# Band attention before two dense layers: scores and outputs by pairs of 64-query units, on keys in place

## The chip, the core and the metric

One kernel runs on one of the eight cores of a Trainium2 chip. The metric is the device time of one execution in microseconds; lower is better. The engines of the core work side by side, each through its own queue in order: PE (matmuls; PEld is its weight loads), ACT, DVE and POOL (elementwise work) and SP, which here issues all DMAs.

## What is computed

`reference()` is attention of two batches, eight heads, 768 positions, head size 64, followed by two feed-forward layers on 1536 tokens of 512 channels. Each query sees the keys less than 16 positions away, and besides 24 summary keys: the maximum over each block of 32 keys, with the mean of the 32 values.

```python
k_sum = k.reshape(B, H, nb, block, D).max(axis=3)
v_sum = v.reshape(B, H, nb, block, D).mean(axis=3)
scores_l = np.where(np.abs(pos[:, None] - pos[None, :]) < 16, scale * q @ k.T, -1e9)
scores_s = scale * q @ k_sum.T + np.log(block)
a = softmax(concat([scores_l, scores_s])); attn = a @ concat([v, v_sum])
x = ((x @ w_a) * (x @ w_b)) @ w_out          # 512 -> 1536 -> 512
h = x @ w_in; out = (h - np.tanh(h)) @ w_out2  # 512 -> 2048 -> 512
```

The five weight matrices arrive as 64-bit floats.

## The kernel before

**Dense part.** Tokens go in three blocks of 512. Every operand of a dense product is split into a high and a low fp32r part, and a product of 128 rows of contraction is three matmuls of 512 columns. A list `pos` of positions, 12 matmuls each, is the backbone: per block and slice f of 128 hidden channels `pos_a`, `pos_b` and, one slice later, `pos_o` (positions 0 to 35 are block 0, 36 to 71 block 1); then `pos_h` and `pos_o2` for the second layer. A weight unit (512 KB of 64-bit words) is loaded into one of five buffers (`stage` three times, `x21a`, `x21b`), rebuilt as fp32 by two ACT copies (`dec_a`), a clamp on POOL and three DVE operations (`dec_b`), and split by one ACT and one DVE or POOL operation (`split_w`). `dec_b` issues the load of the next unit as it frees a buffer.

**Attention.** A unit u is 64 queries of all heads; a pair m is units 2m and 2m+1. `T1` transposes 128 queries and writes them as a block diagonal `qbd`: the two heads of a head pair p sit in the two halves of the rows and of the columns, zeros elsewhere, which takes two half copies. `W` copies a unit's 96 keys and the 24 summary keys to a tile `kw`, side by side. `T2m` makes a unit's scores, one 128 x 128 by 120 product for each p; rows 0 to 63 of the result are one head, rows 64 to 127 the other. `T2s`/`tt`, `ex` add the mask and take exponentials with their sums, `T2b`/`rb`, `nm` divide, `T3` transposes, `T4` multiplies by the values with eight 64-column products a unit and writes x, high part on ACT and low part on DVE.

**Order.** Units 0 to 7, the weights of positions 0 to 2 and the loads for them come first, in an order written by hand, the string `SEQ` (`LK`, `Lq`, `Lv`, `LV`, `Lw` are loads on SP; `da` to `df` rebuild a weight, `sh` and `sl` split it, `vc` copies the value means to a unit's value tile). Units 8 to 23 are planned into blocks 0 and 1 (`plan(j, ...)`), a unit every four positions. For positions below 72 a scheduler sets the order on PE, ACT, DVE and POOL, with attention given priority; SP keeps the order in which the program was written. A unit's values lie in `vw`, three buffers from unit 8 on: `load_v(u+3)` is planned right behind `T4(u)`, which frees its buffer, and what SP issues after it stands behind it.

Of the kernel before, what the change touches and what calls it, by code (L numbers as in the profile page):

```python
# [11 lines left out]
F32 = mybir.dt.float32  # L12
# [3 lines left out]
AF = mybir.ActivationFunctionType  # L16
# [23 lines left out]
def band_attention_moe_kernel(ctx: ExitStack, tc: tile.TileContext, q, k, v, w_a, w_b, w_out, w_in, w_out2, out):  # L40
# [36 lines left out]
    qbd2 = st([128, 2, NP, 128], "wsp", 4)  # L77
# [3 lines left out]
    qbd4 = st([128, 2, NP, 128], "wsp", 4)  # L81
    qbd3 = xb[:, 3072:4096].rearrange("p (u x c) -> p u x c", u=2, x=NP)

    def constants():
        nc.vector.memset(bsq, -math.sqrt(GA) * GB)
        nc.vector.memset(bth, -GC2)
        nc.vector.memset(qbd2, 0.0)
        nc.gpsimd.memset(qbd3, 0.0)
# [11 lines left out]
        nc.gpsimd.memset(qbd4, 0.0)  # L100
        for m, off in zip(masks, (0, WIN, 2 * WIN)):
# [89 lines left out]
    kwb = [st([128, NP, NK], "kw", 2) for _ in range(2)]  # L191
    kwb += [st([128, NP, NK], "w", 3 * F1) for _ in range(2)]
# [4 lines left out]

    def kw_of(u):
        if 8 <= u < 12:
            if u not in kwx:  # L200
                kwx[u] = st([128, NP, NK], "w", 3 * F1)
            return kwx[u]
        return kwb[u % 4 if u < 8 else u % 2]
# [61 lines left out]
    def T1(m, tag, qt):  # L265
        t = qn.pop(m)
        pp = pt(tag, (128, NP, 128))
        for p in range(NP):
            nc.tensor.transpose(pp[:, p, :], t[:, 2 * p : 2 * p + 2, :], ident)
        for h in range(2):  # L270
# [3 lines left out]
        for r in range(2):  # L274
            qb[2 * m + r] = qt[:, r]

    def W(u):
        b, w, k0 = where(u)
        kw = kw_of(u)
        nc.scalar.activation(kw[:, :, 0:KW], kt[b][:, :, k0 : k0 + KW], AF.Copy)  # L280
        if u < 14:
            nc.scalar.activation(kw[:, :, KW:NK], kt[b][:, :, S : S + NB], AF.Copy)

    def T2m(u, tag):
        qt, kw = qb.pop(u), kw_of(u)
        pp = pt(tag, (128, NP, 128))
        for p in range(NP):
            mm(pp[:, p, 0:NK], qt[:, p, :], kw[:, p, :], start=True, stop=True)  # L288
        at_x[u] = pp

    def T2s(u):
        b, w, k0 = where(u)
        pp = at_x[u]
        e = st([128, NP, NK], ("e", "ta", "tg")[u % 3] if u < 8 else "e", 2)
        nm = st([128, NP], "nm", 4)
        sm = st([128, NP], "sm", 4)
        mk = masks[0 if w == 0 else (2 if w == S // 64 - 1 else 1)]
        for p in range(NP):
            nc.vector.tensor_tensor_reduce(
                out=e[:, p, :], in0=pp[:, p, 0:NK], in1=mk, scale=-SC, scalar=3.0e38,  # L300
# [5 lines left out]
        at_x[u] = (e, sm)  # L306

    def T2(u, tag):
        T2m(u, tag)
        T2s(u)  # L310

    def T2b(u):
        e, sm = at_x[u]
        nc.vector.tensor_scalar(sm, sm, 1e-9, None, op0=ALU.add)
        nc.vector.reciprocal(sm, sm)
        if u % 2:
# [4 lines left out]
        at_x[u] = e  # L321

    def T3(u, tag, eng="act"):
        e = at_x.pop(u)
# [3 lines left out]
        at = st([NK, NP, 128], ("at", "gh", "gl")[u % 3] if u < 8 else "at", 2)  # L328
        if eng == "act":
            nc.scalar.activation(at, pp[0:NK], AF.Copy)  # L330
        else:
            nc.vector.tensor_copy(at, pp[0:NK])
        at_x[u] = at

    def T4(u, tag):
        at, vt = at_x.pop(u), vw_of(u)
        pp = pt(tag)
        for p in range(NP):
            for h in range(2):
                mm(  # L340
                    pp[h * 64 : (h + 1) * 64, p * 64 : (p + 1) * 64], vt[:, 2 * p + h, :], at[:, p, h * 64 : (h + 1) * 64],
                    start=True, stop=True,
                )
        x = X[u // 8]
        c0 = (u % 8) * 64
        src = pp[:, 0:256].rearrange("x (p c) -> x p c", p=NP)
        nc.scalar.activation(x[:, 0, :, c0 : c0 + 64], src, AF.Copy)
        nc.vector.tensor_tensor(x[:, 1, :, c0 : c0 + 64], src, x[:, 0, :, c0 : c0 + 64].bitcast(F32), op=ALU.subtract)  # L348
# [202 lines left out]
    for n, u in enumerate(range(8, 24)):  # L551
        j = (n - 8) * 4 + begin[1] + OFF if n >= 8 else n * (begin[1] // 8) + OFF
        b, w, _ = where(u)
        if u % 2 == 0:
            m = u // 2
            if m + 2 < 12:
                plan(j, load_q, m + 2)
            plan(j, T1, m, "pt", qbd)
            if u >= 12:
                plan(j, W, u)  # L560
                plan(j, W, u + 1)
        if u % 8 == 0:
            plan(j, new_x, u // 8)
        plan(j + 2, T2, u, "ps")
        plan(j + 3, T2b, u)
        plan(j + 5, T3, u, "pt")
        plan(j + 7, T4, u, "ps")
        if u + 3 < 24:
            plan(j + 7, load_v, u + 3)
            if 12 <= u + 3 < 15:  # L570
                plan(max(j + 7, VM + NC + 5), load_vm, u + 3)
# [263 lines left out]
```

## Time and profile before

| | us |
|---|---|
| median of three runs (lowest, highest) | 660.85 (659.47, 661.19) |
| the profiled execution | 659.97 |
| its span, from first to last instruction | 658.2 |
| PE busy, share | 637.4, 97% |
| DVE, ACT, POOL busy | 501.9, 475.1, 209.1 |
| mean granted PE clock | 0.995 of full |

The page's chain that ended last is 83% PE and 8% DVE. Its slices show PE at nine tenths or more from the fourth on, except one; DMA is near full over the first 100 us and near nothing after 365 us. A matmul's end is modelled, so the distance from one matmul's start to the next is the better measure of what PE spends.

### The profile page before, as it was taken

What the parts mean: (1) busy time and instruction counts of PE and PEld (TensorE: products, weight loads), DVE (VectorE), ACT (ScalarE), POOL (GpSimd) and SP (SyncE); (2) the same over time, 40 slices, a digit from 0 to 9 for tenths busy, and PEclk for the clock granted to TensorE, in tenths of its full rate; (3) what the DMA queues carried; (4) which work ended last, traced back from release to release, by engine and by line L of the source; (5) the groups of instructions that cost most, each with busy time, mean ns of one, the idle gap of its engine ahead of it and who ended that gap; (6) DMA issues with size and microseconds to landing.
All of it is one profiled execution on the core that took longest, in us unless ns stands there. A gap on an engine that the chain in (4) does not pass through costs nothing.

```text
span 658.2 us, 9626 instructions
## 1 busy us (share of the span) xinstructions
PE 637.4 (97%) x3240; PEld 518.2 (79%) x3240; DVE 501.9 (76%) x999; ACT 475.1 (72%) x1000; POOL 209.1 (32%) x221
## 2 busy tenths in 40 slices
PE   7779999999799999999999999999999999999997
PEld 5567876888588888888888888888888888888885
DVE  5889999898675777747877749777777877777775
ACT  4899886897686787645655548777777777777774
POOL 6752231222000011100111134554444554444441
PEclk9979999999999999999999999999999999999999
DMA  9996984563324554513444200000010000010001
GB/s 203 242 240 185 249 224 127 176 214 116 81 89 124 164 161 141 154 54 113 143 145 145 80 1 0 1 0 1 1 64 1 0 1 0 26 40 1 1 0 64
DMA packets 84781, 62.11 MB, mean 94 GB/s; under 512 B 51892, under 2 KB 75444, under 8 KB 84732
## 3 DMA queue, kind: packets, MB, share of 16 engines
q1 hardware_dynamic: 84732, 61.50, 33.3%
q8 instruction: 25, 0.41, 0.3%
q14 instruction: 24, 0.20, 0.1%
HBM read 54.00 MB, written 7.34 MB: 93 GB/s over the span
## 4 chain that ended last, share of the span: by engine, by line
PE 83%; DVE 8%; ACT 4%; DMA 2%; issue 2%; SPq 1%; POOL 0%; DVEq 0%; ACTq 0%
PE acc L459 20%; PE pb L370 18%; PE pa L370 17%; PE acc L398 12%; PE pt L370 5%; PE ps L370 5%; PE ps L288 1%; DVE w L164 1%; PE ps L340 1%; DVE wsp L185 1%; DMA stage<-in_moe_w_in_dram 1%; DVE w L165 1%; PE pt L240 1%; PE pt L327 1%; SPq L610 1%
## 5 line engine op out<-in xcount | busy, mean ns | idle before, releaser
L185 POOL TENSOR_TENSOR wsp<-w,wsp 128x512 fp32r<-128x512 f32 x97 | 127.4, 1330 | 140.0 <-ACT wsp L184 140.0
L184 ACT ACTIVATE wsp<-w 128x512 fp32r<-128x512 f32 x201 | 121.3, 622 | 17.8 <-PE acc L398 8.0
L185 DVE TENSOR_TENSOR wsp<-w,wsp 128x512 fp32r<-128x512 f32 x104 | 73.9, 712 | 41.0 <-ACT wsp L184 40.8
L179 POOL TENSOR_SCALAR w<-w 128x512 f32<-128x512 f32 x52 | 41.8, 809 | 181.7 <-ACT w L154 168.9
L398 PE MATMUL acc<-gh,wsp 128*128 128x512 f32 x288 | 96.5, 394 | 1.2 <-ACT gh L363 1.2
L370 PE MATMUL pa<-XA,wsp 128*128 128x512 f32 x336 | 85.2, 402 | 2.1 <-ACT XA L720 2.1
L370 PE MATMUL pb<-XA,wsp 128*128 128x512 f32 x336 | 83.9, 393 | 1.4 <-DVE tg L386 1.4
L459 PE MATMUL acc<-wsp,gh 128*128 128x512 f32 x256 | 78.8, 389 | 0.0
L370 PEld LDWEIGHTS pa<-XA,wsp 128*128 128x128 f32 x336 | 64.1, 193 | 16.6 <-ACT XA L720 2.4
L370 PEld LDWEIGHTS pb<-XA,wsp 128*128 128x128 f32 x336 | 62.1, 188 | 14.9 <-ACT x21a L155 1.7
L363 ACT ACTIVATE gh<-tg 128x512 fp32r<-128x512 f32 x68 | 42.4, 624 | 33.9 <-DVE tg L386 33.6
L398 PEld LDWEIGHTS acc<-gh,wsp 128*128 128x128 f32 x288 | 53.7, 188 | 11.9 <-ACT gh L363 1.3
L370 PE MATMUL pb<-XB,wsp 128*128 128x512 f32 x240 | 60.8, 396 | 0.0
L370 PE MATMUL pa<-XB,wsp 128*128 128x512 f32 x240 | 60.0, 394 | 0.0
L398 PE MATMUL acc<-gl,wsp 128*128 128x512 f32 x144 | 56.8, 396 | 1.1 <-DVE gl L364 1.1
L459 PEld LDWEIGHTS acc<-wsp,gh 128*128 128x128 f32 x256 | 48.1, 188 | 9.9
L364 DVE TENSOR_TENSOR gl<-tg,gh 128x512 fp32r<-128x512 f32 x68 | 46.8, 688 | 9.1 <-ACT gh L363 8.9
L370 PEld LDWEIGHTS pa<-XB,wsp 128*128 128x128 f32 x240 | 44.5, 188 | 9.4 <-DVE XB L348 0.2
L370 PEld LDWEIGHTS pb<-XB,wsp 128*128 128x128 f32 x240 | 44.4, 188 | 9.2
L459 PE MATMUL acc<-wsp,gl 128*128 128x512 f32 x128 | 49.8, 389 | 0.0
L459 PE MATMUL acc<-wsp,vw 128*128 128x512 f32 x192 | 46.5, 391 | 0.0
L459 PEld LDWEIGHTS acc<-wsp,vw 128*128 128x128 f32 x192 | 35.9, 188 | 8.2 <-ACT vw L363 0.4
(304 smaller groups left out, 1175.5 us busy)
## 6 DMA issues: line engine op xcount, KB each, us to landing
stage<-in_moe_w_out_dram SPq DMA_DIRECT2D x19, 512.0 KB, 3.5
stage<-in_moe_w_in_dram SPq DMA_DIRECT2D x16, 512.0 KB, 5.6
stage<-in_moe_w_a_dram SPq DMA_DIRECT2D x8, 512.0 KB, 5.0
w<-wsc SPq DMA_DIRECT2D x16, 256.0 KB, 3.4
vw<-in_v_dram SPq DMA_DIRECT2D x19, 192.0 KB, 3.0
stage<-in_moe_w_b_dram SPq DMA_DIRECT2D x7, 512.0 KB, 5.6
wsc<-x21a SPq DMA_DIRECT2D x8, 256.0 KB, 5.1
wsc<-x21b SPq DMA_DIRECT2D x8, 256.0 KB, 4.9
```

The lines of the kernel that those rows point to most:

```text
L164: nc.vector.scalar_tensor_tensor(r, t[:, :, 1], -0x40000000, r, op0=ALU.bitwise_and, op1=ALU.bitwise_or)
L165: nc.vector.tensor_tensor(r, r, t[:, :, 0], op=ALU.add)
L179: nc.gpsimd.tensor_scalar(rf, rf, HI_HI, HI_LO, op0=ALU.min, op1=ALU.max)
L184: nc.scalar.activation(s[:, 0, :], r, AF.Copy)
L185: eng.tensor_tensor(s[:, 1, :], r, s[:, 0, :].bitcast(F32), op=ALU.subtract)
L240: mm(pp, mavg[:, NB - 4 - 4 * c : 2 * NB - 4 - 4 * c], vch.pop(c).rearrange("p h d -> p (h d)"), start=(c == 0), stop=(c == NC - 1),)
L288: mm(pp[:, p, 0:NK], qt[:, p, :], kw[:, p, :], start=True, stop=True)
L363: nc.scalar.activation(dst[0], src, AF.Copy)
L364: eng.tensor_tensor(dst[1], src, dst[0].bitcast(F32), op=ALU.subtract)
L370: mm(dst, w, xx, start=(kk == 0 and n == 0), stop=(kk == KC - 1 and n == 2))
L398: mm(acc[blk][d][:, c0:c1], w, t, start=(f == 0 and c0 == 0 and n == 0), stop=(f == F1 - 1 and n == 2))
L459: mm(a[c], g[:, cs], s[:, i, :], start=(f == 0 and n == 0), stop=(f == F2 - 1 and n == 2))
```

## The change

- **Plain q copies.** `T1` writes the transposed queries with one copy of 128 x 512; the zeroed block-diagonal buffers and their memsets go.
- **Scores on keys in place.** `T2m` now works on a pair. A product is 64 rows (one head) by 64 columns (one unit's queries) by keys; heads go to two PSUM banks, units to the two halves of their rows. Keys are read from the transposed keys `kt` themselves, so that a unit needs two products, 96 keys and 24 summary keys. `W` stays for units 8 to 11 alone (`kwx`), with one product of 120.
- **By head, not by unit.** After `T2m` a tile of 128 rows holds one head of both units. `T2s`, `T2b`, `T3` run for (m, h) instead of u; their number is the same. Masks are made for pairs.
- **T4 and x by 128 tokens.** One bank takes a pair's sixteen products; one ACT and one DVE operation of 512 write x, instead of two of 256 each.
- **First order.** `SEQ` is new. Loads of weights stand among those of attention; the engine of several steps changes, and all `df` and `sl` of the first three weights go to POOL. `load_v` comes in twos behind `T4(m)`.

```diff
+    def q_of(m):
+        return qbx[:, m - 2] if m in (2, 3) else qbd[:, m % 2]
-    def T1(m, tag, qt):
+    def T1(m, tag):
...
-        for h in range(2):
-            r = slice(h * 64, h * 64 + 64)
-            dst = qt[r, :, :, h * 64 : h * 64 + 64]
-            nc.scalar.activation(dst, pp[r].rearrange("x p (u c) -> x u p c", u=2), AF.Copy)
+        nc.scalar.activation(q_of(m), pp, AF.Copy)
...
-        for p in range(NP):
-            mm(pp[:, p, 0:NK], qt[:, p, :], kw[:, p, :], start=True, stop=True)
+                if 2 * m + n in kwx:
+                    parts.append(((0, NK, kwx[2 * m + n]),))
+                else:
+                    parts.append(((0, KW, kt[b][:, :, k0 : k0 + KW]), (KW, NK, kt[b][:, :, S : S + NB])))
+            for i in range(len(parts[0])):
+                for h in range(2):
+                    r = slice(h * 64, h * 64 + 64)
+                    for n in range(2):
+                        c0, c1, keys = parts[n][i]
+                        mm(
+                            pp[h][n * 64 : n * 64 + 64, p, c0:c1], qt[r, p, n * 64 : n * 64 + 64], keys[r, p, :],
+                            start=True, stop=True,
+                        )
...
+    def T4m(m, tag):
+        at = [at_x.pop((m, h)) for h in range(2)]
+        pp = pt(tag, (128, NP, 128))
+        for n in range(2):
+            vt = vw_of(2 * m + n)
+            c = slice(n * 64, n * 64 + 64)
+            for p in range(NP):
+                for h in range(2):
+                    mm(pp[h * 64 : (h + 1) * 64, p, c], vt[:, 2 * p + h, :], at[h][:, p, c], start=True, stop=True)
+        return pp
...
+        x, c0 = X[m // 4], (m % 4) * 128
+        nc.scalar.activation(x[:, 0, :, c0 : c0 + 128], pp, AF.Copy)
...
-    for n, u in enumerate(range(8, 24)):
-        j = (n - 8) * 4 + begin[1] + OFF if n >= 8 else n * (begin[1] // 8) + OFF
+    for n, m in enumerate(range(4, 12)):
+        j = (n - 4) * 8 + begin[1] + OFF if n >= 4 else n * 2 * (begin[1] // 8) + OFF
...
+        plan(j + 9, T4, m, "ps")
+        for u in (2 * m + 3, 2 * m + 4):
+            if u < 24:
+                plan(j + 9, load_v, u)
...
-    T3E, WE, ADD, SPL, VCE = 'DDDDADDD', 'PPDPPDPP', 'PDD', 'PPD', 'APPPAPDD'
+    T1E, T3E, ADD, SPL, VCE = 'AADD', 'ADDDDAAA', 'PPP', 'PPP', 'DDDDPDPP'
```

Three places of the order. SP in the first order, before: the last value loads (`w`, `vw` from `in_v`), then the first weights.

```order
L620 DMA XA<-in_v_dram 128x8x128 x3
L258 DMA w<-in_v_dram 96x8x64 x5
L258 DMA vw<-in_v_dram 96x8x64 x3
L141 DMA stage<-in_moe_w_a_dram 128x4x256
L141 DMA stage<-in_moe_w_b_dram 128x4x256
```

The same place after:

```order
L620 DMA XA<-in_v_dram 128x8x128 x2
L246 DMA w<-in_v_dram 96x8x64
L138 DMA stage<-in_moe_w_b_dram 128x4x256
L246 DMA w<-in_v_dram 96x8x64 x3
L138 DMA stage<-in_moe_w_a_dram 128x4x256
L246 DMA w<-in_v_dram 96x8x64
L246 DMA vw<-in_v_dram 96x8x64 x2
L138 DMA stage<-in_moe_w_b_dram 128x4x256
L246 DMA vw<-in_v_dram 96x8x64
L140 DMA x21a<-in_moe_w_out_dram 128x1024
```

The last value load of the first eight units now stands behind the fourth weight load, the second one from `w_b`, which takes the first `stage` buffer again and so waits until `df0` has emptied it.

PE in block 0, before: a `T2` (L288), a `T4` (L340) and what stands around them.

```order
L398 MATMUL acc_884<-gh,wsp 128x512
L288 MATMUL ps<-kw,qbd 128x120 x4
L398 MATMUL acc_885<-gh,wsp 128x512
L370 MATMUL pb<-XA,wsp 128x512 x9
L340 MATMUL ps<-at,vw 64x64 x8
L370 MATMUL pb<-XA,wsp 128x512 x3
```

After, the scores of pair 6 begin as follows, and a `T4` stands in two parts:

```order
L287 MATMUL pt<-kt,qbd 64x96 x2
L287 MATMUL pt<-kt,qbd 64x24 x2
L376 MATMUL pb<-XA,wsp 128x512 x9
L332 MATMUL pt<-ident,e 120x128 x4
L345 MATMUL ps<-at,vw 64x64
L345 MATMUL ps<-at,vw 64x64 x15
```

Scores of a pair are now 32 products of 64 columns' weights (16 for pairs 4 and 5) in place of eight of 128. They stand in one piece, except for pairs 5 and 6, which are in two; `T4` of seven pairs is in two pieces, 1 and 15 products.

SP toward the end of block 0, before: a value load (L258) stands behind `T4` of one unit, and behind it the last weights of the first layer.

```order
L143 DMA x21b<-in_moe_w_out_dram 128x1024
L258 DMA vw<-in_v_dram 96x8x64
L143 DMA stage<-in_moe_w_out_dram 128x1024
L141 DMA stage<-in_moe_w_in_dram 128x4x256 x2
L258 DMA vw<-in_v_dram 96x8x64
```

After:

```order
L138 DMA stage<-in_moe_w_a_dram 128x4x256
L246 DMA vw<-in_v_dram 96x8x64 x2
L138 DMA stage<-in_moe_w_b_dram 128x4x256
L140 DMA x21a<-in_moe_w_out_dram 128x1024
L140 DMA x21b<-in_moe_w_out_dram 128x1024
L138 DMA stage<-in_moe_w_in_dram 128x4x256 x3
L246 DMA vw<-in_v_dram 96x8x64 x2
```

Two value loads now wait together for `T4` of pair 6, and three weights that block 0 still needs (for positions 33, 34 and 35) stand behind them; before it was one, for position 35, behind `T4` of unit 13.

## Rows read from the trace of the kernel before

**Rows 1.** Span and granted PE clock of the core.

```profile
core 0: 658.2 us, clock 0.995
```

**Rows 2.** Stretches: start:end, length, busy us (count) of each engine, clock, DMA share.

```profile
40.00:60.00 20.00, 16.43 (x68) 12.63 (x67) 17.88 (x35) 18.94 (x46) 6.53 (x8) 0.83 0.94 242
60.00:80.00 20.00, 20.00 (x116) 16.56 (x115) 18.41 (x40) 17.11 (x37) 4.05 (x6) 1.00 0.84 205
...
160.00:200.00 40.00, 36.56 (x204) 29.22 (x203) 26.34 (x70) 28.05 (x71) 3.09 (x5) 1.00 0.31 89
```

**Rows 3.** PE's timeline: start, length, group, [idle before <-what ended it].

```profile
42.48 5.74 PE L370 MATMUL pa<-XA,wsp 128*128 128x512 f32 x12 [2.11 <-ACT XA L720]
...
57.37 2.99 PE L370 MATMUL pb<-XA,wsp 128*128 128x512 f32 x12 [1.44 <-DVE tg L386]
...
169.93 1.21 PE L398 MATMUL acc<-gh,wsp 128*128 128x512 f32 x4 [1.21 <-ACT gh L363]
```

**Rows 4.** PE's timeline around a T2 and a T4, and in the second layer.

```profile
83.72 1.05 PE L288 MATMUL ps<-w,qbd 128*128 128x120 f32 x8
84.52 2.98 PE L370 MATMUL pa<-XA,wsp 128*128 128x512 f32 x12
87.34 0.61 PE L370 MATMUL pb<-XA,wsp 128*128 128x512 f32 x2
87.89 0.69 PE L340 MATMUL ps<-at,vw 120*64 120x64 f32 x16
88.50 2.56 PE L370 MATMUL pb<-XA,wsp 128*128 128x512 f32 x10
90.90 0.39 PE L398 MATMUL acc<-gh,wsp 128*128 128x512 f32 x1
...
501.25 2.88 PE L370 MATMUL pb<-XA,wsp 128*128 128x512 f32 x12
503.97 0.61 PE L459 MATMUL acc<-wsp,gh 128*128 128x512 f32 x2
```

**Rows 5.** PE's timeline in the first order: a T2 and two T4 in a row.

```profile
13.60 1.12 PE L288 MATMUL pt<-kw,qbd 128*128 128x120 f32 x8 [0.25 <-ACT qbd L599]
...
36.73 0.67 PE L709 MATMUL ps<-w,vw 120*64 120x64 f32 x16
37.20 0.67 PE L709 MATMUL pt<-gl,w 120*64 120x64 f32 x16
```

**Rows 6.** Timelines of DVE and POOL late in the first order.

```profile
37.20 1.13 DVE L757 SCALAR_TENSOR_TENSOR w<-stage,w 128x512 int32<-128x512 int32 x1
40.77 0.69 DVE L757 SCALAR_TENSOR_TENSOR w<-stage,w 128x512 int32<-128x512 int32 x1
42.46 0.42 DVE L722 TENSOR_TENSOR XA<-pb,XA 128x256 fp32r<-128x256 f32 x1 [1.00 <-ACT XA L720]
36.41 1.38 POOL L737 TENSOR_SCALAR w<-w 24x512 f32<-24x512 f32 x2
38.47 1.29 POOL L759 TENSOR_TENSOR w<-w,stage 128x512 int32<-128x512 int32 x1 [0.68 <-POOL w L737]
```

**Rows 7.** DMA issues by line: count, size of one, median us to landing.

```profile
vw<-in_v_dram SPq DMA_DIRECT2D x19, 192.0 KB, 3.0
stage<-in_moe_w_b_dram SPq DMA_DIRECT2D x7, 512.0 KB, 5.6
```

**Rows 8.** SP's own waits: us in total, times, longest.

```profile
SPq L258 <- PE ps L340: 112.6, 11, 20.5
```

**Rows 9.** Chain of waits ahead of 168 us: start, us, what.

```profile
156.28 6.25 DMA stage<-in_moe_w_in_dram
```

**Rows 10.** Groups by line and form: busy us, mean ns of one, idle before.

```profile
L280 ACT ACTIVATE kw<-kt 128x384 f32<-128x384 f32 x12 | 6.2, 517 | 0.0
L273 ACT ACTIVATE qbd<-pt 64x512 f32<-64x512 f32 x16 | 9.4, 590 | 0.9 <-PE pt L269 0.8
```

More of the change, by code (lines that the diff above doesn't have):

```diff
@@ L76, in band_attention_moe_kernel @@
     qbd = st([128, 2, NP, 128], "qbd")
-    qbd2 = st([128, 2, NP, 128], "wsp", 4)
+    for _ in range(4):
+        st([128, 2, TB], "wsp", 4)
     xb = st([128, 2 * KC * TB], "XB")
     kq = xb[:, 0:3072].rearrange("p (c h d) -> p c h d", c=NC, h=H)
-    qbd4 = st([128, 2, NP, 128], "wsp", 4)
-    qbd3 = xb[:, 3072:4096].rearrange("p (u x c) -> p u x c", u=2, x=NP)
+    qbx = xb[:, 3072:4096].rearrange("p (u x c) -> p u x c", u=2, x=NP)
     def constants():
@@ new lines, in W, with T2m @@
+        nc.scalar.activation(kwx[u][:, :, 0:KW], kt[b][:, :, k0 : k0 + KW], AF.Copy)
+        nc.scalar.activation(kwx[u][:, :, KW:NK], kt[b][:, :, S : S + NB], AF.Copy)
+    def T2m(m, tags):
+        qt = q_of(m)
+        pp = [pt(t, (128, NP, 128)) for t in tags]
+        for p in range(NP):
+            parts = []
+            for n in range(2):
+                b, w, k0 = where(2 * m + n)
+                if 2 * m + n in kwx:
[12 more added lines that the diff above has]
+        for h in range(2):
+            at_x[m, h] = pp[h]
@@ L305, in T2s, with T2, T2b @@
             )
[L306 to L313, printed above, removed]
+        at_x[m, h] = (e, sm)
+    def T2(m, tags):
+        T2m(m, tags)
+        for h in range(2):
+            T2s(m, h)
+    def T2b(m, h):
+        e, sm = at_x[m, h]
         nc.vector.tensor_scalar(sm, sm, 1e-9, None, op0=ALU.add)
         nc.vector.reciprocal(sm, sm)
-        if u % 2:
+        if h:
             nc.vector.tensor_tensor(e, e, sm.unsqueeze(2).to_broadcast([128, NP, NK]), op=ALU.mult)
@@ L327, in T3, with T4 @@
             nc.tensor.transpose(pp[0:NK, p, :], e[:, p, :], ident)
[L328 to L337, printed above, removed]
-        for p in range(NP):
[L339 to L348, printed above, removed]
+        at = st([NK, NP, 128], "at", 2)
+        nc.scalar.activation(at, pp[0:NK], AF.Copy)
+        at_x[m, h] = at
+    def T4m(m, tag):
+        at = [at_x.pop((m, h)) for h in range(2)]
+        pp = pt(tag, (128, NP, 128))
+        for n in range(2):
+            vt = vw_of(2 * m + n)
+            c = slice(n * 64, n * 64 + 64)
+            for p in range(NP):
+                for h in range(2):
+                    mm(pp[h * 64 : (h + 1) * 64, p, c], vt[:, 2 * p + h, :], at[h][:, p, c], start=True, stop=True)
+        return pp
+    def T4(m, tag):
+        pp = T4m(m, tag)
+        x, c0 = X[m // 4], (m % 4) * 128
+        nc.scalar.activation(x[:, 0, :, c0 : c0 + 128], pp, AF.Copy)
+        nc.vector.tensor_tensor(
+            x[:, 1, :, c0 : c0 + 128], pp, x[:, 0, :, c0 : c0 + 128].bitcast(F32), op=ALU.subtract
+        )
     xtag = ["XA", "XB"]
@@ L550, in band_attention_moe_kernel @@
     OFF = -2
-    for n, u in enumerate(range(8, 24)):
-        j = (n - 8) * 4 + begin[1] + OFF if n >= 8 else n * (begin[1] // 8) + OFF
[L553 to L571, printed above, removed]
+    for n, m in enumerate(range(4, 12)):
+        j = (n - 4) * 8 + begin[1] + OFF if n >= 4 else n * 2 * (begin[1] // 8) + OFF
+        if m + 2 < 12:
+            plan(j, load_q, m + 2)
+        plan(j, T1, m, "pt")
+        if m % 4 == 0:
+            plan(j, new_x, m // 4)
+        plan(j + 2, T2, m, ("ps", "pt"))
+        for h in range(2):
+            plan(j + 3 + h, T2b, m, h)
+            plan(j + 5 + 2 * h, T3, m, h, "pt")
+        plan(j + 9, T4, m, "ps")
+        for u in (2 * m + 3, 2 * m + 4):
+            if u < 24:
+                plan(j + 9, load_v, u)
+                if 12 <= u < 15:
+                    plan(max(j + 9, VM + NC + 5), load_vm, u)
     for d in range(KC):
@@ L701, in op @@
             cp(T3E[i], t, P_["T3", i][0:NK])
[L702 removed]
+            at_x[divmod(i, 2)] = t
         elif n.startswith("T4m"):
             i = int(n[3])
[L705 to L713 removed]
+            P_["T4", i] = T4m(i, tg())
         elif n.startswith("T4"):
```

109 lines of the change are left out of this document (33 added, 76 removed).

## The prediction

> **What bounds the kernel now.** I read the span and clock first. The span is 658.2 us [rows 1], the profiled execution 659.97, so 1.8 lie around it, and that execution is 0.9 under the median of 660.85, well inside the runs. Then the table of stretches [rows 2]: PE is busy for 20.00 of 20.00 us from 60 to 80. From 40 to 60 it is idle for 3.57, at a granted clock of 0.83, and from 160 to 200 it is idle for 3.44; the slices of the page show no other hole after the head. So from about 57 us the kernel costs what PE issues, plus one gap. ACT (17 to 19 of 20 us) and DVE (18) are nearly full in block 0, but PE does not wait for them except in that gap, which begins with gh of ACT [rows 3]. Before 57 us PE is mostly a server of the attention chain, and the end of that head is set by when x of the first 512 tokens is complete: pa(0) starts at 42.48 behind ACT writing `XA`, pb(1) at 57.37 [rows 3].
>
> A matmul's end is modelled, so I price PE by distances of starts. Twelve matmuls of 512 columns take 503.97 − 501.25 = 2.72 us, 0.227 each, 0.444 ns a column [rows 4]. A `T2` among them: 84.52 − 83.72 = 0.80, and the twelve behind it need 87.34 − 84.52 = 2.82 instead of 2.72; the visit costs 0.90. A `T4`: from 87.34 to 90.90 are twelve pb and one `T4`, 3.56 − 2.72 = 0.84. Two `T4` in a row start 0.47 apart for 16 instructions [rows 5], 29 ns each, which is 64 columns at 0.444. So of a visit's 0.84, 0.47 is products and 0.37 is the way into the small form and out of it. The same rows show each fp32 product as two passes: 16 instructions for eight products.
>
> **Part one: PE after the head.** This is where every microsecond counts in full.
>
> Scores of pairs 6 to 11 are 32 products, 64 passes. The 32 passes of 96 columns take 96 × 0.444 = 43 to 44 ns, 1.40 us. The 32 of 24 columns would take 11 ns by columns, but each needs its own weights of 64 columns, and the shortest cadence with new weights in the trace is the 29 ns of `T4` [rows 5]; I take 29, 0.93 us. With 0.37 for the visit that is 2.70 a pair, against two visits of 0.90 = 1.80: +0.90 for each of six, **+5.4**.
>
> Pairs 4 and 5 have 32 passes of 120 columns, 54 ns each: 1.74 + 0.37 = 2.11 against 1.80, twice, **+0.6**. Two visits of scores are split in two (pairs 5 and 6): **+0.7**.
>
> `T4`: before 16 visits of 0.84, 13.4. After 8 × 32 × 29 ns = 7.5, and 15 visits (seven are split) of 0.37 = 5.6, together 13.1: **−0.4**.
>
> Sum **+6.3**. Transposes keep their number. Bounds of the one unknown, the cadence of these products: by columns alone the short passes give back 0.59 a pair, −3.5, so +2.8; if two neighbours ran fully at once, products halve (6 × 1.17 + 2 × 0.87 = 8.7), −2.4; if each pass waited for its weights as long as it runs, products double, +17.5, so +23.8. I take the middle value because `T4` [rows 5] is nearest: 64 columns of weights, fp32, small form, in one order on one engine.
>
> **Part two: what is hidden.** ACT loses most of the unit copies `W` (12 of them, 6.2 us [rows 10]) and half of its copies of q (16 of 0.59, 9.4 us [rows 10], become 8 of a little more), and writes x once a pair: some 10 us of ACT in the main part, and a little of DVE. PE at 20.00 of 20.00 hides all of it; I cost it at nothing, and would count it only where ACT is the last releaser, in the gap at 168. Masks and sums by head instead of by unit are as many and as long. If that cover were gone, in the head, it counts there.
>
> **Part three: the head.** I walked the new first order through instruction by instruction, each on its engine in order, each waiting for its operands, with the durations of its line before; the same walk on the old order gives pa(0) at 42.3 where the trace has 42.48, so it is good to a few tenths. A score visit is 2.3 there (a row of `T2` starts as early as 13.60 [rows 5]). The steps that decide: four score pairs take about 9.3 us of PE, more than eight visits did, but the exponentials end within 0.2 us of where they did, since ACT and DVE are the slower part. All `df` go to POOL, 1.29 instead of 0.69 [rows 6]. That costs on POOL and frees DVE, with one more cost shown by the rows: a DVE operation that runs beside a POOL one takes 1.13 at 37.20 while POOL's 36.41 + 1.38 is under way, and 0.69 at 40.77 [rows 6]. In the walk `df0` ends at 35.3.
>
> The queue: the last value load now stands on SP behind a weight load that waits for `df0` to empty `stage`. So it is issued at about 35.3. The weight load alone takes 5.6 and the value load 3.0 [rows 7]; two together 4.7 by my estimate, bounds 3.0 (no contention) and 8.6 (one after the other). It lands at 40.0; unit 7's `T4`, 42.2; its high part on ACT, 42.8; its low part on DVE, 43.5 (before: 42.46 + 0.42 = 42.9 [rows 6]). pa(0) thus starts at **43.5 to 43.6**, 1.1 later. The twelve matmuls of pa(0) took 5.74 [rows 3], in part waiting for the split weights; at half clock 512 columns are 0.43, twelve 5.1. The split weights are all ready earlier now, `sl0` at 40.2, so that wait goes. Behind it pb(0), the next pa, scores of pair 4, and pb(1) at **56.4** against 57.37 [rows 3], with about the same PE work ahead of it: −1.0. Half of that I give to the error of the walk: **−0.5**, between −3 (the value load early, the clock full) and +4 (the value load last).
>
> **Part four: the gap at 168.** SP waited for 112.6 us in 11 times for `T4` before a value load, the longest 20.5 [rows 8], and what stands behind is held with it: a weight of w_in issued at 156.28 landed 6.25 later [rows 9]. Now two value loads and behind them the weights of positions 33, 34 and 35 wait for `T4` of pair 6, which stands at position 29.6 in PE's order; before, one weight, for position 35, waited for `T4` of unit 13 at 30.8. From there to position 33 are 3.4 positions of 2.72 and about 3 us of visits: some 12.5 us. The weight needs 6.25 to land and seven steps of decoding and splitting of 0.69 each [rows 6], 4.8: 11.1. Just in time; I leave the gap of 3.44 [rows 2] as it is.
>
> **Forecast:** 659.97 + 6.3 − 0.5 = **665.8**, by the profiled execution; its own range, by the cadence and the head, is 661.5 to 669.
>
> **The rivals.**
>
> *Four products at once* (faster). A product fills a quarter of the array, and neighbours use other quarters. The point from which it decides: a cadence under 22 ns averaged over the 64 passes of a pair ((1.80 − 0.37) / 64) would take the price below that of two `T2`. At half the cadence PE after the head gains 8.7 on the forecast, the head 1.9: **655.2**. Against it: `T4`'s neighbours already lie in two column halves [rows 5], and their starts are 64 columns apart, no less. The Trainium skill, "TensorEngine Tiling (Array Packing)", section "Key Properties", says that different tiles load and multiply in parallel; by that rule this rival would be the forecast, but the 29 ns do not show it for `T4`. Chance 0.13.
>
> *The paired value loads starve block 0* (slower). If the two value loads, 3.0 each [rows 7], go ahead of the weight one after the other, position 33 is ready after 6.0 + 6.25 + 4.8 = 17.0 us against 12.5: PE stands 4.5 more near 165 to 172 us, **670.3**. It decides if the weight is not split 12.5 us after `T4` of pair 6. For it: the longest waits are of this line [rows 8]. Against: DMA is at 0.31 there [rows 2]. Chance 0.18.
>
> *Loads of one row half do not overlap* (slower still). Both products of a head use the same 64 rows; if weights for a half of the rows only load when its products are done, three of four loads show: 0.75 × 17.5 = 13, **679**. Against it: `T4`'s weights all lie in the same rows and come every 29 ns [rows 5]. The Trainium skill, "TensorE: Matmul & The Clock Gate", section "The mechanism", says that weight loads overlap running products only where the row group differs; the 29 ns speak against that. Chance 0.06.
>
> *The gap closes and the clock holds* (same). With ACT some 10 us lighter gh is no longer late at 169.93 [rows 3], −3.4; and if PE, which has more to do in the head, keeps its full clock into pa(0) (before, half level from 41.6 to 48.4, the 0.83 of rows 2), twelve matmuls gain 12 × 0.2 = 2.4: **660.0**. One of the two alone leaves 662.4 or 663.4. For it: ACT is named as what ended that gap. Against it: its weights come through the same SP queue. Chance 0.20.
>
> **How the numbers follow.** Forecast 0.43, four at once 0.13, starved 0.18, no overlap 0.06, gap and clock 0.20. A measurement of this kernel can tell about 0.3% from no change, so same is 658.9 to 662.8. Slower: 0.58, of the forecast 0.34 and the two slower rivals, 0.18 and 0.06. Faster: 0.22, four at once and 0.09 of the last rival, below its figure. Same: 0.20, the other 0.11 of that rival and 0.09 at the low end of the forecast. The range runs from 655, four at once, to 674, the starved case with a cadence above mine; above it lies little but no overlap.
>
> **What would show it.** In the changed kernel's profile: starts of 64 x 96 products 44 ns and of 64 x 24 products 29 ns apart, and 2.7 us from a pair's first score product to the next dense one. Halved distances make the first rival, doubled ones the third. pa(0) should start at 43 to 44.5 and pb(1) at 56 to 57.5; a later pa(0) must name the last value load. The idle time from 160 to 200 should be 3 to 4 us; 8 would be the starved case, with a weight named behind SP's wait for `T4`, under 1 the last. PE's busy time should rise by about 6. The forecast is wrong if PE's sum over visits moves by less than 3, or if a new gap opens before 57 us, such as a POOL queue that delays the first weights.

## The result, and the profile after

The changed kernel takes 669.59 us (median of four, 669.27 to 670.47) against 660.91 of the kernel before measured with it: ratio 1.0138, 95% interval 1.012 to 1.0156. It is slower, inside the forecast range (655 to 674), by 8.7 us. The profiled execution took 669.90, against 659.97 before: 9.9 more, where the forecast, made from that execution, had 5.8.

The span, and three stretches (start:end, length, busy us and count of each engine, granted clock, DMA share), which answer to [rows 1] and [rows 2]:

```profile
core 0: 668.2 us, clock 0.986
```

```profile
40.00:60.00 20.00, 18.04 (x118) 14.25 (x115) 16.08 (x39) 16.47 (x43) 8.65 (x9) 0.91 1.04 252
60.00:80.00 20.00, 18.90 (x115) 14.06 (x114) 17.85 (x34) 17.34 (x34) 5.50 (x6) 1.00 0.78 195
...
160.00:200.00 40.00, 34.21 (x224) 27.07 (x223) 29.07 (x73) 30.32 (x80) 4.58 (x8) 0.91 0.47 134
```

Before, PE had no idle time from 60 to 80 us; now it is idle for 1.10 there, and for 5.79 instead of 3.44 from 160 to 200, where the clock is now 0.91 as well. Only the head has less idle time, 1.96 from 40 to 60 instead of 3.57.

PE executes the same 2448 dense matmuls in the same order in both kernels, so the start of every twelfth gives a common scale, the position. Worked out from the two traces:

| | before | after | difference |
|---|---|---|---|
| position 0 starts | 42.48 | 42.43 | −0.05 |
| position 4 starts | 60.55 | 56.94 | −3.6 |
| positions 4 to 36 (block 0) | 116.7 | 124.7 | +7.9 |
| positions 36 to 72 (block 1) | 117.3 | 122.9 | +5.6 |
| position 72 to the end | 363.7 | 363.7 | 0.0 |

The head wins, and the two blocks that carry attention lose nearly four times as much. PE's timeline at the two longest gaps (start, length, group, [idle before <-what ended it]):

```profile
163.78 1.75 PE L376 MATMUL pa<-XA,wsp 128*128 128x512 f32 x7
168.65 1.14 PE L376 MATMUL pb<-XA,wsp 128*128 128x512 f32 x2 [3.12 <-ACT wsp L181]
...
186.56 2.65 PE L376 MATMUL pb<-XB,wsp 128*128 128x512 f32 x11
191.88 1.43 PE L376 MATMUL pa<-XB,wsp 128*128 128x512 f32 x4 [2.67 <-ACT ta L384]
```

The first waits for a weight (position 33), the second for `ta`, a copy of pa that stands on ACT behind exponentials. Both are followed by 3.4 us at half clock (the granted clock is 0.5 from 168.8 to 172.2 and from 192.7 to 196.1). The chain of waits into the first gap (start, us, what):

```profile
152.97 1.09 PE ps L345 x30
...
154.69 0.41 SPq L138
...
155.21 6.32 DMA x21a<-in_moe_w_out_dram
...
161.61 0.68 ACT w L151
162.29 0.57 ACT x21a L152
162.86 1.52 ACT e L307 x8
```

and ACT's timeline over the same time:

```profile
155.44 0.60 ACT L384 ACTIVATE ta<-pa 128x512 f32<-128x512 f32 x1 [0.76 <-PE pa L376]
160.26 0.67 ACT L151 ACTIVATE w<-stage 128x512 f32<-128x512 f32 x1 [4.22 <-DMA stage<-in_moe_w_b_dram]
...
162.76 0.38 ACT L307 ACTIVATE e<-e,nm 128x120 f32<-128x120 f32 x1
...
167.98 0.61 ACT L181 ACTIVATE wsp<-w 128x512 fp32r<-128x512 f32 x1
```

`T4` of pair 6 ends at 154; behind it SP issues the two value loads and then the weights that had stood behind them. ACT stands idle for 4.22 us with the copy of such a weight first in its queue. The scores of pair 7 were begun on PE at 156.91, but their exponentials stand behind that copy and start at 162.76; the high part of the weight for position 33 comes behind both, at 167.98. DVE waits in the same way: its last step on this weight (L162) stands behind an operation on the softmax's sums, which waits for those exponentials.

```profile
164.41 0.17 DVE L319 TENSOR_SCALAR sm<-sm 128x4 f32<-128x4 f32 x1 [0.88 <-ACT e L307]
...
164.83 0.68 DVE L162 CUSTOM_DVE_ANT_0 w<-stage,w 128x1024 uint16<-128x1024 uint16 x1
```

The weight is whole at 165.5, and ACT takes it 2.5 us later, behind copies of other weights. This is the chain of the starved case. SP's waits for `T4`, which answer to [rows 8], are fewer and shorter in sum than before, and the longest is nearly as long:

```profile
SPq L246 <- PE ps L345: 69.9, 6, 18.5
```

Score products are the surprise on the other side. A whole visit of a pair on keys in place:

```profile
240.89 0.61 PE L404 MATMUL acc<-gh,wsp 128*128 128x512 f32 x2
241.44 0.68 PE L287 MATMUL pt<-kt,qbd 64*64 64x96 f32 x13
...
243.00 0.25 PE L287 MATMUL ps<-kt,qbd 64*64 64x24 f32 x4
243.18 0.50 PE L404 MATMUL acc<-gl,wsp 128*128 128x512 f32 x1
243.51 0.63 PE L404 MATMUL acc<-gh,wsp 128*128 128x512 f32 x2
```

1.74 from the first score product to the next dense matmul, 0.10 lost behind it and 0.09 ahead: 1.94 us, where the prediction had 2.70 and two old visits cost 1.80. Four of the five whole visits in place measure 1.94 to 1.96 us, one 1.75. The order within a visit is part of it: in the four, products of one head alone run for the first 0.50 us, in the one for 0.32, before the other head's join them. On copies, 16 products of 120 columns run in fours:

```profile
51.46 0.27 PE L287 MATMUL ps<-w,qbd 64*64 64x120 f32 x2
51.48 0.27 PE L287 MATMUL pt<-w,qbd 64*64 64x120 f32 x2
51.56 0.27 PE L287 MATMUL ps<-w,qbd 64*64 64x120 f32 x2
51.58 0.27 PE L287 MATMUL pt<-w,qbd 64*64 64x120 f32 x2
51.78 2.60 PE L376 MATMUL pa<-XA,wsp 128*128 128x512 f32 x10
```

Four passes in 0.10 us, some 25 ns each; that whole visit, worked out the same way, costs 1.20.

### The profile page after: what moved, and what is told of

Read it like the earlier page. It is cut to its first block, busy times and chain, and to the rows that moved or that the text cites. A ratio compares the mean times of both kernels' runs of the same rounds, so it can differ in the third digit from the quotient of the medians.

```text
span 668.2 us, 10552 instructions
## 1 busy us (share of the span) xinstructions
PE 643.2 (96%) x3752; PEld 519.9 (78%) x3752; DVE 496.0 (74%) x975; ACT 462.9 (69%) x965; POOL 207.5 (31%) x215
## 4 chain that ended last, share of the span: by engine, by line
PE 76%; DVE 10%; ACT 6%; DMA 4%; SPq 2%; issue 1%; POOL 0%; ACTq 0%; DVEq 0%; POOLq 0%
PE acc L465 20%; PE pa L376 16%; PE pb L376 16%; PE acc L404 11%; PE pt L376 5%; PE ps L376 5%; DVE w L162 2%; DVE w L161 2%; ACT e L307 1%; DVE wsp L182 1%; PE ps L345 1%; DMA x20b<-in_q_dram 1%; ACT w L151 1%; DMA x21a<-in_moe_w_out_dram 1%; DMA w<-in_v_dram 1%
## 5 line engine op out<-in xcount | busy, mean ns | idle before, releaser
L369 ACT ACTIVATE gh<-tg 128x512 fp32r<-128x512 f32 x68 | 42.3, 622 | 35.3 <-DVE tg L392 35.1
L404 PEld LDWEIGHTS acc<-gh,wsp 128*128 128x128 f32 x288 | 53.7, 188 | 12.5 <-DVE wsp L182 1.4
L152 ACT ACTIVATE stage<-stage 128x512 int32<-128x512 uint32 x47 | 31.6, 672 | 24.6 <-DMA stage<-in_moe_w_in_dram 16.1
```

The lines of the kernel that those rows point to most:

```text
L152: nc.scalar.activation(t[:, :, 0], t[:, :, 0].bitcast(U32), AF.Copy, scale=2.0 ** -29)
L369: nc.scalar.activation(dst[0], src, AF.Copy)
L404: mm(acc[blk][d][:, c0:c1], w, t, start=(f == 0 and c0 == 0 and n == 0), stop=(f == F1 - 1 and n == 2))
```

## The experiments

The theory after the result: block 0 loses because two value loads hold the weights behind them on SP (A). Its rivals: the pair's exponentials in one burst (B), PE's own work, or another engine that paces block 0 (D). The numbers of positions in the table at the end are worked out from each trace as above.

Two things limit what the runs can show. In every run but one (the exponentials of head 1), the scheduler's order on PE, ACT and DVE changed together with the edit, so none of these runs changes one thing alone. And that one run kept the order of every engine and still took 127.3 us for positions 4 to 36, where the changed kernel took 124.7: between two profiled executions, differences of this size are no evidence.

**Order of the score products.** Head and unit become the outer loops, so that neighbours lie in the same quarter of the array.

```diff
-        for p in range(NP):
-            parts = []
+        for h in range(2):
+            r = slice(h * 64, h * 64 + 64)
             for n in range(2):
                 b, w, k0 = where(2 * m + n)
...
-            for i in range(len(parts[0])):
-                for h in range(2):
...
-                    for n in range(2):
...
+                for p in range(NP):
...
+                    for c0, c1, keys in parts:
```

> The changed kernel with the score products of one head and one unit in a row, so that neighbours lie in the same quarter of the array. If the measured 25 ns per pass come from neighbours in four quarters that run at once: a pass then takes what it takes alone, by the rate of the old scores (0.80 us for 8 passes of 120 columns, 0.8 ns a column) 78 ns for 96 columns and at least 20 to 29 for 24, a visit 3.4 to 3.8 us in place of 1.94, +9 to +11 us in the main part and some more in the head: 680 to 685. If passes run one after another as the prediction assumed, the order of quarters does not matter: 669 to 671, visit 1.9 to 2.0.

Measured 690.92 (two runs, 687.45 and 694.38), ratio 1.046 (1.040 to 1.052). A visit:

```profile
195.75 0.40 PE L373 MATMUL pb<-XB,wsp 128*128 128x512 f32 x1
196.07 1.73 PE L284 MATMUL pt<-kt,qbd 64*64 64x96 f32 x25
...
199.66 2.81 PE L373 MATMUL pa<-XB,wsp 128*128 128x512 f32 x11
```

3.59 us instead of 1.74 for the same 64 passes, 56 ns each instead of 27; the five whole visits lie from 3.58 to 3.85. So products of different quarters do run at once, and the prediction's one-after-the-other falls. The time is above the expected 680 to 685: it cost 11 us in the head (position 0 starts at 53.56), where the granted clock stood at half from 24.7 to 38.4. The run also gave something that it was not made for: from position 4 to 36 PE has some 4 us more to do than in the changed kernel (visits of scores 5.0 more, eight key transposes fewer), and the stretch takes 124.9 instead of 124.7, with 3.6 us of idle time instead of 5.9 and no half clock. That speaks against PE's own work as what sets block 0. It is no clean test, since PE reached position 4 later by 13.6 us, a lead for the other engines.

**Copies of the keys for all units.**

```diff
-        kwx[u] = st([128, NP, NK], "w", 3 * F1)
+        kwx[u] = st([128, NP, NK], "w", 3 * F1) if u < 12 else st([128, NP, NK], "kw", 2)
...
         plan(j, T1, m, "pt")
+        if m >= 6:
+            plan(j, W, 2 * m)
+            plan(j, W, 2 * m + 1)
```

> The changed kernel with W for all units, so that a score is one product of 120 columns instead of 96 and 24. The two copied pairs show 1.2 us a visit against 1.94 for keys in place, so six pairs give PE back 4.4 us; ACT gets 24 copies more, some 8.5 us. If ACT's work as such sets the gaps: no gain or slower, 669 to 673. If the gaps are due to when weights land (theory A), the gaps stay as they are and the time is 665 to 667.

669.12 (668.58 to 670.77), ratio 1.0127 (1.011 to 1.0144): nothing gained. The expected 1.2 us a visit did not come, since twelve of its visits are halves of 16 passes, one bank each, which cost 1.17: two quarters alone, and the way in and out paid twice. The gap at 189 went, the one at 165 grew to 4.7. The time is where the first reading (ACT's work sets the gaps) put it, but since PE got no work back it does not decide between the two.

**Value loads later on SP.**

```diff
-                plan(j + 9, load_v, u)
+                plan(j + 15, load_v, u)
...
```

> The changed kernel with the two value loads behind T4(m) written six positions later, all else alike. Theory A (the pair of value loads holds the weight loads behind it on SP, ACT's next operation is a copy of such a weight, and exponentials that are ready stand behind it): the gaps at 165 us (3.3 us) and 189 us (2.8 us) and the two stretches at half clock (3.4 us each) go, idle of PE from 160 to 200 falls from 5.8 to under 2, time 661 to 664. Rival B (the exponentials of a pair come in one burst and ACT has no room for the weights, whenever they land): the weights land earlier, the gaps stay within 1 us, time 667 to 670.

672.31 (670.72 to 672.99), ratio 1.0175 (1.0156 to 1.0193), above both expectations. The weight of position 33 was issued at 136.7 instead of 154.6 and split 8 us earlier, and the gap at 165 went. Others took its place; PE's timeline:

```profile
134.45 3.00 PE L376 MATMUL pb<-XA,wsp 128*128 128x512 f32 x12 [0.77 <-DVE tg L392]
138.38 1.20 PE L404 MATMUL acc<-gh,wsp 128*128 128x512 f32 x4 [0.93 <-ACT gh L369]
160.40 1.32 PE L287 MATMUL ps<-kt,qbd 64*64 64x96 f32 x22 [2.20 <-DVE XB L352]
193.94 4.62 PE L376 MATMUL pa<-XB,wsp 128*128 128x512 f32 x12 [3.14 <-ACT ta L384]
```

The third is of the same kind as before with other actors. On ACT x of pair 6, whose products ended at 154, stands behind copies of second-layer weights that wait for their loads:

```profile
152.02 0.68 ACT L152 ACTIVATE stage<-stage 128x512 int32<-128x512 uint32 x1 [2.41 <-DMA stage<-in_moe_w_in_dram]
...
155.97 0.67 ACT L152 ACTIVATE stage<-stage 128x512 int32<-128x512 uint32 x1 [2.24 <-DMA stage<-in_moe_w_in_dram]
...
159.05 0.57 ACT L351 ACTIVATE XB<-ps 128x512 fp32r<-128x512 f32 x1
```

The granted clock then stood at half from 160.9 to 167.7, twice as long as after each gap of the changed kernel. Here A as the whole cause falls: with that weight early, positions 4 to 36 take 125.0, as long as in the changed kernel.

**Five value buffers.** The loads stay where they are and wait for a `T4` long done.

```diff
-    vwb = [st([NK, H, D], "vw", 3) for _ in range(3)]
+    vwb = [st([NK, H, D], "vw", 3) for _ in range(3)] + [st([NK, H, D], "kw", 2) for _ in range(2)]
-        return vwx[u] if u < 5 else vwb[u % 3]
+        return vwx[u] if u < 5 else vwb[u % 3 if u < 12 else (u - 9) % 5]
...
```

> The changed kernel with two more buffers for the values of units from 12 on, so that the two value loads wait for the T4 of the pair before, which is long done; places in the program unchanged. Theory A1 (SP's wait for T4 as such is the loss of block 0): SP's waits on T4 fall from 70 us to under 20, the gaps at 165 and 189 go and nothing takes their place, 661 to 664. Theory A2 (block 0 is bound by the chain of attention and weight decoding on ACT and DVE, whose orders are fixed; freeing one load moves the gap, as the run with later loads did): SP's waits go, but the time is 667 to 671.

673.42 (670.86 to 674.05), ratio 1.0187 (1.0155 to 1.0218). SP's waits for `T4` fall from 69.9 us to 7.2, with 2.2 more in the first order; among what is left are waits for weight buffers:

```profile
SPq L140 <- DVE w L162: 78.5, 20, 12.0
...
SPq L138 <- DVE w L162: 46.7, 17, 6.8
...
SPq L246 <- PE ps L345: 7.2, 2, 5.9
```

Block 0 takes 126.3. The gap at 165 is gone, and PE waits instead at 144 (ACT `at`, 0.79), 159 (ACT `qbd`, 1.26), 161 (DVE `XB`, 1.12) and 194 (ACT `e`, 3.00); the granted clock is at half from 160.3 to 167.1 and from 194.5 to 197.9. A1 falls: the waits went and the time did not. A2 had that right, though the time is 2.4 above its range; that ACT and DVE are the reason is not shown by this run.

**The same, with the second layer's weights decoded two positions later.**

```diff
-            ja = begin[1] + 2 + 2 * early.index(u)
+            ja = begin[1] + 4 + 2 * early.index(u)
```

> As the run with five value buffers, and besides the decoding of the second layer's weights (not needed before position 72) begins two positions later. In the run with later loads x of pair 6 stood on ACT behind copies of such weights, which waited for their loads (2.41 and 2.24 us), and PE behind it for 2.3. If these copies are what takes the gap's place (A2): 2 to 4 us less than the run with five buffers. If the attention chain itself is late: within 1 us of it.

673.36 (672.11 to 674.11), ratio 1.0191: no difference to five buffers alone, as expected if the attention chain itself is late. But it may also be that two positions are not enough; the run does not tell which.

**The kernel before with value loads in twos.**

```diff
-            plan(j + 7, load_v, u + 3)
+            for w_ in ((u + 2, u + 3) if u % 2 else ()):
+                plan(j + 7, load_v, w_)
```

> The kernel before with one thing of the change: value loads in twos behind the T4 of every second unit, at the place the changed kernel has them. If the pairing of loads is what costs block 0 (theory A1): weights of positions 33 to 36 land some 10 us later, 664 to 667. If it is not (A2): 660 to 662.

666.29 (665.61 to 666.90), ratio 1.0085 (1.0068 to 1.0103): 5.4 us for this part, with the order that comes with it. Block 0 loses 1.3, block 1 3.5. The gap of [rows 3], at 169.93 there, is now a wait for a weight and twice as long:

```profile
172.21 0.50 PE L398 MATMUL acc<-gh,wsp 128*128 128x512 f32 x1 [2.35 <-ACT wsp L184]
```

So pairing the loads costs the old kernel about what the starved case said (4.5), but mostly not where it said: PE's idle time from position 4 to 36 stays at 3.4 us, and what is new (2.5 us) lies in block 1. SP's waits for `T4` even fall, from 112.6 us [rows 8] to 53.2 in 6 times. In the changed kernel the same hold is there, and neither run that lifts it is faster.

**T4, x and value loads by unit in the changed kernel.**

```diff
-        plan(j + 9, T4, m, "ps")
+        plan(j + 8, T4u, m, 0, "ps")
+        plan(j + 9, T4u, m, 1, "ps")
...
```

> The changed kernel with T4, the two writes of x and the value load by single unit again, one position apart; scores stay by pairs. If T4 and x by pairs hold the bank ps and the value loads too long: gaps from 60 to 200 us fall by 3 or more, 664 to 667. If it is the pair's softmax chain in one piece (16 operations on ACT and DVE per score visit) that comes late: 669 to 672, a little slower for the extra operations on ACT and DVE.

705.00 (702.29 to 706.75), ratio 1.0668: far outside both expectations. The loads wait more often and longer:

```profile
SPq L246 <- PE ps L358: 127.2, 12, 24.4
```

The weight of position 32 is issued at 167.5 instead of 134.7, and block 0 takes 142.3, block 1 136.2. It is no clean reversal of that part, since the order of all engines moved with it, so what of the 35 us is due to what stays open.

**The kernel before with loads later.**

```diff
-            plan(j + 7, load_v, u + 3)
+            plan(j + 12, load_v, u + 3)
...
```

> The kernel before with each value load written five positions later, still by single units. If its one gap, at 168 us, comes from the weight behind the value load on SP: the gap goes and the time is 656.5 to 658.5. If, as in the changed kernel, another queue then sets the same time: 660 to 664.

661.89 (ten runs, 659.96 to 662.66), ratio 1.0017 (1.0003 to 1.0031). The gap at 168 went (block 0 in 115.1 instead of 116.7), and block 1 lost 4.2: waits of 0.85 (ACT `XB`), 1.13 and 0.88 (ACT `e`) took its place. The gain of 2 to 4 did not come; the time is where the second expectation put it, by which another queue then sets the same time.

**The exponentials of head 1 two positions later.**

```diff
-        plan(j + 2, T2, m, ("ps", "pt"))
+        plan(j + 2, T2m, m, ("ps", "pt"))
+        plan(j + 2, T2s, m, 0)
+        plan(j + 4, T2s, m, 1)
         for h in range(2):
-            plan(j + 3 + h, T2b, m, h)
+            plan(j + 3 + 2 * h, T2b, m, h)
...
```

> The changed kernel with the maxima and exponentials of head 1 planned two positions after those of head 0, instead of in one piece. Theory B (bursts): idle of PE from 60 to 200 us (8.6 us) falls by 3 or more, time 663 to 667. Theory A (weights behind the value loads): within 1 us of the changed kernel, 668.5 to 670.5, as the waits on SP are as before.

670.72 (669.76 to 671.73), ratio 1.0154. The gaps stay, 2.93 us at 170 and 2.51 at 193. But the edit did not reach the engines: in its trace the instructions of PE, ACT, DVE and POOL, and the loads on SP, stand in the order of the changed kernel. The exponentials of a pair still stand in one run on ACT:

```profile
161.66 0.66 ACT L151 ACTIVATE w<-stage 128x512 f32<-128x512 f32 x1 [4.04 <-DMA stage<-in_moe_w_b_dram]
...
164.15 0.38 ACT L307 ACTIVATE e<-e,nm 128x120 f32<-128x120 f32 x1
...
166.43 0.38 ACT L307 ACTIVATE e<-e,nm 128x120 f32<-128x120 f32 x1
```

So this run is a second measurement of the changed kernel's order, and B was not tested: it neither falls nor holds.

**Less ACT work.** The second copy of `dec_a` goes for the first layer, so that the low words of these weights are left out.

```diff
-        nc.scalar.activation(t[:, :, 0], t[:, :, 0].bitcast(U32), AF.Copy, scale=2.0 ** -29)
+        if u >= 3 * F1:
+            nc.scalar.activation(t[:, :, 0], t[:, :, 0].bitcast(U32), AF.Copy, scale=2.0 ** -29)
...
```

> The changed kernel without the ACT copy that scales the low words of a weight, for the first layer's weights decoded in the loop (33 operations of 0.67 us, 22 us of ACT; DVE repeats the operation before in place of the addition, same length). If ACT sets the pace of block 0 (its queue, in which attention stands behind weights): positions 4 to 36 take 118 to 121 us and the time is 662 to 666. If DVE alone does: 668 to 670.

665.06 (664.49 to 665.94), ratio 1.0070 (1.0045 to 1.0095). The time and block 0 are where the first expectation put them: positions 4 to 36 take 119.7 instead of 124.7, twice the difference between the two executions of the same order, and the gap at 165 is gone, while one of 1.88 (ACT `at`) opens at 140. Block 1 gains nothing to speak of (122.4). Idle of PE from 160 to 200 falls from 5.79 to 2.02:

```profile
160.00:200.00 40.00, 37.98 (x243) 29.56 (x243) 28.30 (x64) 26.65 (x63) 5.33 (x5) 0.96 0.35 96
```

**Less DVE work, in both kernels.** The low parts of block 0's weights are left out.

```diff
-        eng.tensor_tensor(s[:, 1, :], r, s[:, 0, :].bitcast(F32), op=ALU.subtract)
+        if lo:
+            eng.tensor_tensor(s[:, 1, :], r, s[:, 0, :].bitcast(F32), op=ALU.subtract)
...
```

> The changed kernel without the DVE operation that makes the low part of a weight, for the weights of block 0 (33 operations of 0.70 us, 23 us of DVE; PE multiplies by the high part a second time instead, so its work is the same). If DVE sets the pace of block 0 (D): positions 4 to 36 take 118 to 121 us instead of 124.7, and the time is 663 to 666. If DVE does not: 668 to 670.

> The kernel before without the same 33 DVE operations. It waits only some 4 us after 57 us, so at most that goes: 657 to 660.5. The distance of the changed kernel without them to this one then is what the change costs without DVE's pace: 3 to 5 us if DVE sets the pace there, 8 to 10 if it does not.

Changed kernel: 667.31, but its runs lie from 664.58 to 670.26, and the profiled one is the slowest; in it block 0 takes 124.9, no less than with the work. Kernel before: 656.57 (656.51 to 657.70), ratio 0.9941 (0.992 to 0.9962), block 0 in 114.8. So 23 us of DVE are worth 3.9 us before; in the changed kernel the profiled execution shows no gain in block 0, while the median gains 2.3. The two kernels lie 10.7 us apart without that work, no less than with it (8.7), which speaks against DVE's work as what the change costs; the wide runs leave that unsettled.

| positions | 4 starts | 4 to 36 | 36 to 72 |
|---|---|---|---|
| before | 60.6 | 116.7 | 117.3 |
| changed | 56.9 | 124.7 | 122.9 |
| changed, same quarter | 70.5 | 124.9 | 126.6 |
| changed, loads later | 57.8 | 125.0 | 124.1 |
| changed, head 1 later (same order) | 55.8 | 127.3 | 123.3 |
| changed, copies for all | 57.4 | 127.5 | 120.5 |
| changed, five buffers | 56.2 | 126.3 | 125.1 |
| changed, five buffers, later weights | 55.7 | 125.4 | 125.7 |
| changed, by unit | 58.4 | 142.3 | 136.2 |
| changed, less ACT | 57.1 | 119.7 | 122.4 |
| changed, less DVE | 57.4 | 124.9 | 122.6 |
| before, loads in twos | 61.4 | 118.0 | 120.8 |
| before, loads later | 60.7 | 115.1 | 121.5 |
| before, less DVE | 59.1 | 114.8 | 117.2 |

No version beats the kernel before with all its work.

## Why the prediction was right, and where not

The direction and the range held. The figure of 665.8 is 3.8 low, and it is the sum of terms that were wrong in both directions. That it came so near is luck: the loss was forecast from the scores, whose extra cost came out at less than a third of its price, and it came mostly from gaps, which were forecast to stay as they were. By its own sign, PE's sum over visits moving by less than 3, the forecast's account was wrong (the sum moved by 2.0). The idle time from 160 to 200, 5.79, lies between its 3 to 4 and the 8 of the starved case.

**Scores: the price was wrong, and the row for it was there.** Forecast: +6.7 (in a sum of +6.3). Measured, from position 4 on: 14 units take 14.4 us (a wait of 0.5 taken out), 1.03 a unit against 0.90, so **+1.8**. The step that failed read the 29 ns of `T4` [rows 5] as one product after another at the dense matmuls' 0.444 ns a column. But the visit of the old `T2` [rows 4] had eight passes of 120 columns in 0.80 us, 0.10 each or 0.8 ns a column: an fp32 pass runs at about half the dense pace, so 64 columns alone take some 52 ns, and `T4`'s 29 ns already were two at once. Read one by one, its starts show it: in the visit at 87.89, two passes start 6 to 7 ns apart, the next two 52 ns after them. The 29 ns are the mean, and the prediction's "their starts are 64 columns apart, no less" does not hold. By that reading, four quarters give 24 ns for 120 columns; 25 are measured. The first rival had the mechanism of the scores right, and its sum, −2.4, is as far from the measured +2.0 as the forecast's +6.3. It put 18 ns on a pass in place; the trace shows 27. Two reasons can be seen in the rows: once both heads' products run, a pass still takes some 22 ns in the mean of 96 and 24 columns, so the short ones do not shrink with their columns; and the first 0.50 us of a visit run with one head, two quarters, alone. The visit with 0.32 of it costs 1.75, a little below two old ones.

**T4: nearly right.** −0.4 forecast. A split pair costs 0.45 with its first products and 1.27 with the rest, 1.72 against two old visits at 0.82: +0.2 in all.

**Head: right in kind, too small.** Position 0 starts where it did (42.43, forecast 43.5). The last value load was issued at 35.29 (forecast 35.3), and `T4` that waited for it ran at 39.79 (40.0); behind it one write of x was later than before but the wait for `sl0` was gone. pb(1) starts at 54.21 (56.4). At position 4 the gain is 3.6; like for like it is some 3.1, as eight key transposes and one `T3` (1.35) now come later and the scores of one unit (0.9) earlier. The half clock around pa(0) lasted 3.4 instead of 6.8 us. Forecast −0.5, measured **−3.1**.

**The gap at 168: this is the term with most of the loss.** The forecast left it at 3.44 and took the 12.5 us from `T4` of pair 6 to position 33 as enough for 11.1. Measured: from the end of `T4` at 154.1 to the split at 169.7 are 15.6 us, since ACT takes the weights of other positions and eight exponentials in between, which the seven steps left out. That is the starved case, at 3.1 us instead of 4.5. It came a second time, at 189, behind `T4` of pair 7, and each time with 3.4 us of half clock. Idle time from 60 to 200 us went from 3.4 to 8.6; by the distances of starts, the gaps over 0.25 us from position 4 on add up to 10.1 against 4.1, +6.0, and the half clock cost the dense matmuls another 2.6.

**The cover.** "PE at 20.00 of 20.00 hides all of it" was true for the kernel before and taken over for the one after. The same row had ACT at 17.1 and DVE at 18.4 of 20 [rows 2]. Of the 7.9 us that block 0 lost, 2.4 are idle time of PE (5.9 instead of 3.4 us), and the half clock with the slow first matmuls behind waits adds some 2.5; the rest, some 3, is PE's work on small products and transposes, part of it moved there out of the head. With the edit and the new order that came with it, PE can be given 4 us more there without loss (same quarter), SP's hold can be lifted without gain (five buffers), and 22 us taken from ACT give 5.0 back. The reading that fits these three is that ACT's queue, with the order fixed in it, paces block 0 of the changed kernel. It is a reading and not shown: that run also shortens each weight's chain by a copy, orders moved in all three, and the burst of exponentials (B) was not tested. It would not be ACT's share of work: from position 4 to 36 ACT is busy for 95.3 us in the old kernel and 95.2 in the new one, in a longer stretch. The 10 us that the prediction took from ACT came off elsewhere, ahead of position 4 and in block 1. At the gap that the rows show, ACT stands with a copy in front whose load is not there. What in the change brought its order out of step (pairs in the plan, the earlier head, or the loads in twos) is not settled: the loads in twos, with their order, cost 5.4 in the old kernel, and undoing their hold in the new one moved the gaps to other places. Block 1's loss of 5.6 stayed at 5 or more in every changed version but the one with copies for all units (3.2), and has no experiment of its own.

**The ledger.** −3.1 (head) + 2.0 (scores and `T4`) + 6.0 (gaps) + 2.6 (clock) = +7.5 of the 9.9 us between the profiled executions. The gaps are counted here by distances of starts, which include the slow first matmuls behind a wait. The other 2.4 lie in many distances of 0.1 to 0.3 us in blocks 0 and 1, which I could not put to one cause.

## What to carry to other kernels

When PE is full over a stretch and ACT and DVE are nearly full too, do not cost a change at PE's work alone: ask for each load that moves which copy waits for it at the front of an in-order queue, and what stands behind that copy. Freeing one such queue may gain only until the next one ends last, so test two before building on either. Where a scheduler sets the order, look in the trace first whether an edit changed it, and how much else moved with it. Price small products from the slowest row of the same type first; a short mean distance between starts may already hide products that run at once, so read the starts one by one.

## What the runs showed of the hardware

Products of 64 rows by 64 columns of weights in the four quarters of the array ran at once: 25 ns a pass of 120 columns when neighbours went to four quarters, 51 when a visit had two of them (two passes every 0.10 us), and 56 against 27 when a pair's products went quarter by quarter. The Trainium skill, "TensorEngine Tiling (Array Packing)", section "Key Properties", states that different tiles load and multiply in parallel; these runs agree.

After waits of PE of 3.1 and 2.7 us the granted clock fell to half for 3.4 us, in the changed kernel twice (from 168.8 and from 192.7; in the head it is at half from 18.6 to 25.4 and from 42.5 to 45.9 besides). In the kernel before it did not fall again between 48.4 us and the last us of the run, where PE was never idle for more than 1.44. The length of the one wait did not decide it: with less ACT work the clock fell at 187.4 behind a wait of 1.02 us, and in the run by unit it stayed full behind one of 2.36 at 100.3.
